# Attention stage of a fused attention and mixture-of-experts kernel: wider fp32 products, clamp and q's product trade engines, loads by chunk

## The chip, the cores and the metric

The kernel runs on one core of one Trainium2 chip. The metric is the device time in microseconds (us) of one execution. The engines of the core are named as in the profile: PE (TensorE: matrix products and transposes), PEld (its weight loads), DVE (VectorE), ACT (ScalarE), POOL (GpSimd) and SP (SyncE, which here issues loads and stores).

## The reference, cut to what matters

A gated linear attention over 4 batches, 8 heads, 768 steps and head size 48 feeds a top-2 mixture of 8 experts (3072 tokens, width 384, inner width 1024), which feeds a feed-forward block with inner width 2048. The attention is the part that the change touches:

```python
f = 1.0 / (1.0 + np.exp(-f_logit))
for t in range(S):
    state = f[:, :, t, :, None] * state + np.einsum('bhd,bhe->bhde', k[:, :, t], v[:, :, t])
    y[:, :, t] = np.einsum('bhd,bhde->bhe', q[:, :, t], state)
```

The rows of y, with the heads side by side, are the tokens x. The logits of the experts are `x @ w_gate + log1p(exp(x @ w_noise)) * noise`; the two largest choose the experts and their weights. An expert is `relu(x @ w1) @ w2`; the last block is `h = x @ w_in; (h - tanh(h)) @ w_out`.

## The kernel before

**Chunks.** The 768 steps are cut into six chunks of 128 for each of four batches: 24 chunks, numbered j, batch fastest. One chunk has f, k and q as [128, 4, 128] tiles (partitions: two heads of 64 rows, 48 of them used; four pairs of heads a; 128 steps) and v as [128 steps, 8 heads, 48]. Per chunk SP loads f (256 KB), kq (512 KB) and v (192 KB).

**The work of one chunk**, by function name. `clamp` bounds f from below (L303; on DVE for the first three chunks, on POOL for the rest). `decay` takes exp and ln on ACT (L310, L311) and a running sum along the steps on DVE (L312). `scaled` takes two exponentials on ACT (L320, L321), multiplies k and q by them on DVE (L323, L325) and copies the last step's decay into `gall` on POOL (L326). `scores` makes the 128x128 products of k and q by head on PE (L338), and DVE masks them into `am` (L340). `key_rows` transposes k on PE (L351), ACT copies it out. `outputs` adds, in PSUM, q times the state (L362, from chunk 4 on) and the masked scores times v (L365), and ACT copies the result to x (L368). `states` makes the product of k and v on PE (L379), DVE adds the old state in two half-partition pieces into `tsum` (L383), POOL multiplies it by the decay into `st` (L384). `x_transposed` and `logits` transpose x and multiply it by the gate weights (L390, L402). The 48 rows of a head's state stand in a 96-column block for each pair of heads; the other half of the block is kept at zero, because the two half sums leave it alone.

**Routing.** After each group of four chunks the generator `route` finds the experts and the slots of its tokens; `advance` runs it in small steps between the other work. It then fills `posts` with eight scatters, two per chunk, that write x to the rows `xs` of the experts. `post(n)` issues up to n of them: each a small memset (L470) and an indirect DMA (L471), both on POOL. At j=19 `post(8)` empties the list, and `load_x` (L153, a POOL DMA) loads the first block of tokens of expert 0.

**Order.** The schedule is written out by hand: each engine runs its instructions in the order of the program and waits at each for its data and its buffers. An iteration j of the main loop (from L498 on) issues the loads of chunk j+3, then `scores(j+1)`, `scaled(j+2)`, `decay(j+3)`, `logits(j-1)`, `outputs(j)`, `key_rows(j+1)`, `states(j)`, `x_transposed(j)`, `clamp(j+4)` and `post(4)`. So on POOL an iteration has the copy for `gall` of chunk j+2, the state product of chunk j, the clamp of chunk j+4 and up to four scatters. Chunks 20 to 23 have no key rows and no new state. In iteration 22 three tiles of the first expert block are transposed (`put_x`, L180), and the first product of an expert (L192) is issued in iteration 23.

PSUM is used by bank names: scores b3 and b4, key rows b1, outputs b5, the key and value product and the warming products b6, logits b7. `warm(n)` issues n small bf16 products (L484) whose result nobody reads; the start has `warm(80)`.

Before the loop the load queue of SP has f of chunks 0 and 1, then for each chunk kq, v and the f two chunks on, the gate weights, and eight writes of zeros (288 KB each, L294) into rows of `xs`. After the loop come the expert stage (L192, L207) and the feed-forward stage (the same lines of products), written out in the same manner.

Of the kernel before, what the change touches and what calls it, by code (L numbers as in the profile page):

```python
# [8 lines left out]
F32 = mybir.dt.float32  # L9
# [14 lines left out]
NT = B * NCH  # L24
# [35 lines left out]
def fast(ctx, tc, flag, f_cols, kq_cols, v_rows, gates, w12, w_in, w_out, out):  # L60
# [34 lines left out]

    gall = consts.tile([128, NT, 4], F32, name="gall")
    yslot = consts.tile([128, 2, NT], I32, name="yslot")
# [154 lines left out]
    with ExitStack() as actx:  # L252
# [11 lines left out]
        def load_all(j):  # L264
            if j < NT:
                t = loads.tile([128, 2, 4, 128], F32, name="kq")
                nc.sync.dma_start(t.rearrange("p n a t -> p (n a t)"), kq_cols[j])
                T["k", j], T["q", j] = t[:, 0], t[:, 1]
                T["v", j] = loads.tile([128, H, D], F32, name="v", bufs=4)
                nc.sync.dma_start(T["v", j].rearrange("p h d -> p (h d)"), v_rows[j])  # L270
            load_f(j + 2)

        load_f(0)
        load_f(1)
        load_all(0)
        load_all(1)
        gn = small.tile([128, GN], F32, name="gn", bufs=1)
        nc.sync.dma_start(gn, gates)
        wgn = gn[:, 0:48].rearrange("p (a c) -> p a c", a=3)
        nz = gn[:, 48:].rearrange("p (c b e) -> p c b e", c=NCH, b=B)  # L280
        load_all(2)

        carry = acst.tile([128, 4, 128], F32, name="carry")
        nc.vector.memset(carry, 1.0)
        nc.vector.memset(carry[:, :, 0:1], 0.0)
        st = acst.tile([128, B, 4, 96], F32, name="st")
        nc.vector.memset(st, 0.0)
        tsum = acst.tile([128, 4, 96], F32, name="tsum")
        nc.vector.memset(tsum, 0.0)
        spare = gath.tile([128, 4, DM], F32, name="x4", bufs=2)  # L290
        empty = spare[:(CAP - FILLED) // 4].rearrange("p a d -> p (a d)")
        nc.vector.memset(empty, 0.0)
        for e in range(NE):
            nc.sync.dma_start(rows(xs, (NE * 512 + e * 320 + FILLED - 512) * DM, [[4 * DM, (CAP - FILLED) // 4], [1, 4 * DM]]),  # L294
                              empty)
# [3 lines left out]
        def clamp(j):  # L299
            if j >= NT:  # L300
                return
            fc = work.tile([128, 512], F32, name="fc")
            (nc.vector if j < 3 else nc.gpsimd).tensor_scalar(fc, T.pop(("f", j)), FMIN, None, op0=OP.max)  # L303
            T["fc", j] = fc
# [9 lines left out]
        def scaled(j):  # L314
            if j >= NT:
# [8 lines left out]
                                           op0=OP.min, op1=OP.mult)  # L324
            nc.vector.tensor_tensor(t[:, 1], eneg, T.pop(("q", j)), op=OP.mult)  # L325
            nc.gpsimd.tensor_copy(gall[:, j, :], eneg[:, :, 127])  # L326
            T["kT", j], T["qT", j] = t[:, 0], t[:, 1]
# [28 lines left out]
        def outputs(j):  # L356
            c, b = divmod(j, B)
            am, qT, vt = T.pop(("am", j)), T.pop(("qT", j)), T["v", j]
            pY = ps.tile([128, H, D], F32, name="pY", tag="b5")
            for a in range(4):  # L360
                if c:
                    nc.tensor.matmul(pY[:, 2 * a:2 * a + 2, :].rearrange("p h d -> p (h d)"), qT[:, a, :],  # L362
                                     st[:, b, a, :], start=True, stop=False)
                for s in range(2):
                    nc.tensor.matmul(pY[:, 2 * a + s, :], am[:, s, a, :], vt[:, 2 * a + s, :],  # L365
                                     start=not c, stop=bool(s) or not c)
            x = xkeep[j // 4 % 3][:, j % 4, :]
            nc.scalar.activation(x, pY.rearrange("p h d -> p (h d)"), AF.Copy)  # L368
            T["x", j] = x

        def states(j):
# [6 lines left out]
            for a in range(4):  # L378
                nc.tensor.matmul(pK[:, a, :], k[:, a, :], vt[:, 2 * a:2 * a + 2, :].rearrange("p h d -> p (h d)"),  # L379
                                 start=True, stop=True)  # L380
            for s in range(2):
                pp, cc = slice(64 * s, 64 * s + 64), slice(48 * s, 48 * s + 48)
                nc.vector.tensor_tensor(tsum[pp, :, cc], pK[pp, :, cc], st[pp, b, :, cc], op=OP.add)  # L383
            nc.gpsimd.tensor_tensor(st[:, b], tsum, gall[:, j, :, None].to_broadcast([128, 4, 96]), op=OP.mult)  # L384

# [12 lines left out]
        def logits(j):  # L398
            p = ps.tile([128, 16], F32, name="pt", tag="b7")
            xT = T.pop(("xT", j))  # L400
            for a in range(3):
                nc.tensor.matmul(p, xT[:, a, :], wgn[:, a, :], start=(a == 0), stop=(a == 2))  # L402
            nc.scalar.activation(lgs[:, j, :], p, AF.Copy)

# [76 lines left out]
        def warm(n):  # L481
            p = ps.tile([128, 512], F32, name="pK", tag="b6")
            for _ in range(n):
                nc.tensor.matmul(p[:, :128], ones, ones, start=True, stop=True)  # L484

        clamp(0)
        decay(0)
        warm(80)
        clamp(1)
        scaled(0)  # L490
        decay(1)
        scores(0)
        key_rows(0)
        scaled(1)
        clamp(2)
        decay(2)
        clamp(3)
        for j in range(NT):  # L498
            load_all(j + 3)
            rate = 2 if j < NT - 1 else 8  # L500
            scores(j + 1)
# [21 lines left out]
            clamp(j + 4)  # L523
            post(4)
            advance(rate)
# [192 lines left out]
    def check_routes():  # L718
        holds(0, gall.rearrange("p a b -> p (a b)"), GMIN, OP.is_ge)
        holds(1, dv, 0.0, OP.is_lt)  # L720
# [327 lines left out]
```

## Time and profile before

| | |
|---|---|
| median of 3 runs | 1092.74 us (1091.09 to 1095.36) |
| profiled execution | 1092.13 us, its span 1090.1 us |
| mean granted clock of TensorE | 0.958 |
| PE busy | 1059.0 us, 97% of the span |
| PEld busy | 980.8 us, 90% |
| DVE busy | 637.4 us, 58% |
| ACT busy | 501.3 us, 46% |
| POOL busy | 183.8 us, 17% |
| moved by DMA | 115.31 MB, mean 106 GB/s |

The profile is of one execution. The span runs from the first to the last instruction. In a row of busy time by stretch the length is followed by the busy us of PE, PEld, DVE, ACT and POOL, each with its number of instructions in parentheses. A matrix product of fp32 operands stands in the trace as two instructions, and so does its weight load; a transpose is one. PEclk, or the granted clock, is the share of TensorE's full clock of 2.4 GHz that was granted in a stretch: 1.00 is 2.4 GHz, 0.50 is 1.2 GHz. In a row of a timeline the first number is the start, the second the duration of the merged instructions, and a bracket gives the engine's idle time before them with what ended it. POOL's scatters count as instructions of POOL; what the DMA moves afterwards does not.

### The profile page before, as it was taken

Reading aid. Unit: us, or ns where it says so; the run is one execution under the profiler, and the core shown is the slowest. Engines: PE = TensorE matmul, PEld = TensorE weight load, DVE = VectorE, ACT = ScalarE, POOL = GpSimd, SP = SyncE. Lnnn points to the kernel's source line nnn. Section 1 sums busy time; section 2 is a strip of 40 time slices with the busy share of each in tenths; the row PEclk is TensorE's granted clock in tenths of the full one; section 3 lists DMA queues with packets and bytes.
Section 4 is the critical chain, followed back from the end, with each engine's and each line's share of the span. In section 5 each row is a group of like instructions: output and inputs, shape, how many; then the busy total and the mean of one; then the engine's idle time right before and its main releaser. Section 6 shows DMA issues by size and latency. Waiting matters only on the chain.

```text
span 1090.1 us, 16283 instructions
## 1 busy us (share of the span) xinstructions
PE 1059.0 (97%) x6170; PEld 980.8 (90%) x6170; DVE 637.4 (58%) x1285; ACT 501.3 (46%) x1017; POOL 183.8 (17%) x246
## 2 busy tenths in 40 slices
PE   7989888999999999999999999999999999999997
PEld 7889887899998989999999998998999989999996
DVE  6866665335555555556666576656655555555543
ACT  4654544233242434334444444554655555555552
POOL 2466666430000000000000011410201101000000
PEclk7988777799999999999999999999999999999998
DMA  8665554253453535354445343310101111000000
GB/s 252 233 213 165 169 187 143 97 152 111 117 185 102 168 108 167 115 170 130 149 119 155 96 143 109 94 30 30 51 13 53 30 37 45 1 29 1 29 1 33
DMA packets 54723, 115.31 MB, mean 106 GB/s; under 512 B 7210, under 2 KB 30510, under 8 KB 54637
## 3 DMA queue, kind: packets, MB, share of 16 engines
q1 hardware_dynamic: 46140, 85.08, 25.2%
q0 software_dynamic: 8496, 29.11, 8.5%
q8 instruction: 51, 0.84, 0.3%
q14 instruction: 36, 0.29, 0.1%
HBM read 84.27 MB, written 29.88 MB: 105 GB/s over the span
## 4 chain that ended last, share of the span: by engine, by line
PE 90%; POOL 5%; DVE 2%; ACT 2%; issue 1%; POOLq 0%; DVEq 0%
PE py L207 39%; PE ph L192 38%; PE pY L365 3%; PE px L180 3%; POOL fc L303 2%; POOL xs L471 2%; PE pA L338 2%; PE pY L362 1%; PE pK L379 1%; PE pt L402 1%; POOL st L384 1%; PE pE L390 1%; PE pkr L351 1%; DVE tsum L383 1%; ACT fc L310 1%
## 5 line engine op out<-in xcount | busy, mean ns | idle before, releaser
L207 PE MATMUL py<-wsplit,hs 128*128 128x384 f32 x2432 | 462.6, 337 | 0.0
L207 PEld LDWEIGHTS py<-wsplit,hs 128*128 128x128 f32 x2432 | 430.1, 188 | 13.2
L192 PE MATMUL ph<-xtH,wsplit 128*128 128x512 f32 (+3 forms) x768 | 230.9, 359 | 2.0 <-ACT xtH L182 1.5
L192 PE MATMUL ph<-xtH,winS 128*128 128x512 f32 x576 | 196.4, 396 | 0.0
L192 PEld LDWEIGHTS ph<-xtH,wsplit 128*128 128x128 f32 x768 | 140.0, 189 | 15.7 <-ACT xtH L182 1.9
L192 PE MATMUL ph<-xtL,wsplit 128*128 128x320 f32 (+3 forms) x384 | 135.3, 352 | 0.0
L619 DVE SCALAR_TENSOR_TENSOR s<-s,z 128x512 f32<-128x512 f32 x96 | 66.5, 692 | 109.8 <-ACT s L618 109.2
L192 PEld LDWEIGHTS ph<-xtH,winS 128*128 128x128 f32 x576 | 108.1, 188 | 20.4
L216 ACT ACTIVATE hs<-ph 128x512 fp32r<-128x512 f32 (+3 forms) x128 | 66.0, 516 | 129.7 <-PE ph L192 103.5
L627 ACT ACTIVATE hs<-g 128x512 fp32r<-128x512 f32 x96 | 60.7, 632 | 140.4 <-DVE g L621 138.9
L220 DVE SCALAR_TENSOR_TENSOR hs<-ph,hs 128x256 fp32r<-128x256 f32 (+2 forms) x192 | 79.6, 443 | 75.7 <-ACT hs L216 69.8
L192 PE MATMUL ph<-xtL,winS 128*128 128x512 f32 x288 | 113.4, 394 | 0.0
L628 DVE TENSOR_TENSOR hs<-g,hs 128x512 fp32r<-128x512 f32 x96 | 66.5, 693 | 63.6 <-ACT hs L627 62.9
L126 DVE TENSOR_TENSOR wsplit<-raw,wsplit 128x768 fp32r<-128x768 f32 x72 | 69.3, 963 | 39.2 <-ACT wsplit L125 38.9
L183 DVE TENSOR_TENSOR xtL<-px,xtH 128x384 fp32r<-128x384 f32 (+1 forms) x80 | 42.8, 536 | 62.5 <-ACT xtH L182 55.3
L192 PEld LDWEIGHTS ph<-xtL,wsplit 128*128 128x128 f32 x384 | 72.7, 189 | 5.8 <-DVE xtL L183 0.3
L617 ACT ACTIVATE z<-ph 128x512 f32<-128x512 f32 x96 | 57.3, 596 | 43.0 <-PE ph L192 41.4
L125 ACT ACTIVATE wsplit<-raw 128x768 fp32r<-128x768 f32 x72 | 60.5, 840 | 27.7 <-DMA raw<-in_w 27.6
L618 ACT ACTIVATE s<-z,bias_a 128x512 f32<-128x512 f32 x96 | 69.7, 726 | 3.1
L182 ACT ACTIVATE xtH<-px 128x384 fp32r<-128x384 f32 (+1 forms) x80 | 37.6, 471 | 72.1 <-PE px L180 71.6
L621 DVE TENSOR_TENSOR g<-s,ph 128x512 f32<-128x512 f32 x96 | 65.9, 687 | 3.3
L153 POOL DMA_DIRECT2D x<-xs x16 | 8.9, 556 | 343.5 <-PE px L180 341.3
(124 smaller groups left out, 1185.1 us busy)
## 6 DMA issues: line engine op xcount, KB each, us to landing
raw<-in_w SPq DMA_DIRECT2D x64, 384.0 KB
kq<-in_kq_cols SPq DMA_DIRECT2D x24, 512.0 KB
y_rows<-yo SPq DMA_DIRECT2D x41, 192.0 KB
f<-in_f_cols SPq DMA_DIRECT2D x24, 256.0 KB
w<-in_moe_w_out SPq DMA_DIRECT2D x32, 192.0 KB
w<-in_moe_w_in SPq DMA_DIRECT2D x24, 256.0 KB
v<-in_v_rows SPq DMA_DIRECT2D x24, 192.0 KB
x<-xs POOLq DMA_DIRECT2D x6, 768.0 KB
```

What stands on the lines that cost most here:

```text
L125: nc.scalar.activation(t[:, 0], raw, AF.Copy)
L126: nc.vector.tensor_tensor(t[:, 1], raw, t[:, 0].bitcast(F32), op=OP.subtract)
L192: nc.tensor.matmul(ph[:, :n], l, r[:, a, :n], start=(o == 0), stop=(o == 8))
L207: nc.tensor.matmul(p[:max(m, 128)], l, r, start=(f == 0 and o == 0), stop=(f == last and o == len(ops) - 1))
L216: nc.scalar.activation(hs[:, :n], ph[:, :n], AF.Relu)
L220: nc.vector.scalar_tensor_tensor(hs[:, at:at + hi - lo], ph[:, lo:hi], 0.0, hs[:, lo:hi].bitcast(F32), op0=OP.max, op1=OP.subtract)
L617: nc.scalar.activation(z, ph, AF.Square, accum_out=hsum[:, i:i + 1])
L618: nc.scalar.activation(s, z, AF.Square, bias=bias_a)
L619: nc.vector.scalar_tensor_tensor(s, s, ZD, z, op0=OP.add, op1=OP.mult)
L621: nc.vector.tensor_tensor(g, s, ph, op=OP.mult)
L627: nc.scalar.activation(hs[:, :512], g, AF.Copy)
L628: nc.vector.tensor_tensor(hs[:, 512:], g, hs[:, :512].bitcast(F32), op=OP.subtract)
```

## The change

**Wider products.** `outputs` streams 144 columns of the state instead of 96, and gives each product of masked scores the 48 columns of v twice, to its own place and to a place that a later product overwrites or nobody reads. `logits` streams 96 columns of the gate tile instead of 16 and copies the first 16. The state of a batch is a tile of its own with 432 columns.

**Engines.** All clamps are on DVE. q's product (L325) is on POOL, ahead of the decay column. The decay column becomes a product with a mask `own`, so that the unused halves of the state blocks are multiplied by zero; the state sum is then one instruction over all partitions.

**Order.** f, kq and v are loaded chunk by chunk; chunk 2 and the gate weights come later in the program. The clearing of the state tiles, the first three clamps and the first decays are put in another order; `warm(10)` stands before the loop and at the top of iterations 1 and 2. The writes of zeros are issued two each in iterations 1 to 4. Up to iteration 19 `post` issues two scatters instead of four.

**Check.** The test of the smallest decay first takes the larger of the two masked columns.

```diff
@@ -93,7 +93,7 @@
 
-    gall = consts.tile([128, NT, 4], F32, name="gall")
+    gall = consts.tile([128, NT, 4, 2], F32, name="gall")
     yslot = consts.tile([128, 2, NT], I32, name="yslot")
@@ -268,29 +268,29 @@
                 nc.sync.dma_start(T["v", j].rearrange("p h d -> p (h d)"), v_rows[j])
-            load_f(j + 2)
+            if j:
+                load_f(j + 1)
 
         load_f(0)
+        load_all(0)
         load_f(1)
-        load_all(0)
         load_all(1)
         gn = small.tile([128, GN], F32, name="gn", bufs=1)
-        nc.sync.dma_start(gn, gates)
         wgn = gn[:, 0:48].rearrange("p (a c) -> p a c", a=3)
         nz = gn[:, 48:].rearrange("p (c b e) -> p c b e", c=NCH, b=B)
-        load_all(2)
 
         carry = acst.tile([128, 4, 128], F32, name="carry")
         nc.vector.memset(carry, 1.0)
         nc.vector.memset(carry[:, :, 0:1], 0.0)
-        st = acst.tile([128, B, 4, 96], F32, name="st")
-        nc.vector.memset(st, 0.0)
-        tsum = acst.tile([128, 4, 96], F32, name="tsum")
-        nc.vector.memset(tsum, 0.0)
+        own = acst.tile([128, 2], F32, name="own")
+        nc.vector.memset(own, 0.0)
+        for s in range(2):
+            nc.vector.memset(own[64 * s:64 * s + 64, s:s + 1], 1.0)
+        st = [acst.tile([128, 432], F32, name=f"st{b}") for b in range(B)]
         spare = gath.tile([128, 4, DM], F32, name="x4", bufs=2)
         empty = spare[:(CAP - FILLED) // 4].rearrange("p a d -> p (a d)")
-        nc.vector.memset(empty, 0.0)
-        for e in range(NE):
+
+        def clear(e):
             nc.sync.dma_start(rows(xs, (NE * 512 + e * 320 + FILLED - 512) * DM, [[4 * DM, (CAP - FILLED) // 4], [1, 4 * DM]]),
@@ -300,7 +300,7 @@
             fc = work.tile([128, 512], F32, name="fc")
-            (nc.vector if j < 3 else nc.gpsimd).tensor_scalar(fc, T.pop(("f", j)), FMIN, None, op0=OP.max)
+            nc.vector.tensor_scalar(fc, T.pop(("f", j)), FMIN, None, op0=OP.max)
             T["fc", j] = fc
@@ -322,8 +322,9 @@
                                            op0=OP.min, op1=OP.mult)
-            nc.vector.tensor_tensor(t[:, 1], eneg, T.pop(("q", j)), op=OP.mult)
-            nc.gpsimd.tensor_copy(gall[:, j, :], eneg[:, :, 127])
+            nc.gpsimd.tensor_tensor(t[:, 1], eneg, T.pop(("q", j)), op=OP.mult)
+            nc.gpsimd.tensor_tensor(gall[:, j], eneg[:, :, 127:128].to_broadcast([128, 4, 2]),
+                                    own[:, None, :].to_broadcast([128, 4, 2]), op=OP.mult)
             T["kT", j], T["qT", j] = t[:, 0], t[:, 1]
@@ -356,16 +357,19 @@
             am, qT, vt = T.pop(("am", j)), T.pop(("qT", j)), T["v", j]
-            pY = ps.tile([128, H, D], F32, name="pY", tag="b5")
+            pY = ps.tile([128, 512], F32, name="pY", tag="b5")
+
             for a in range(4):
+                at = 96 * a
                 if c:
-                    nc.tensor.matmul(pY[:, 2 * a:2 * a + 2, :].rearrange("p h d -> p (h d)"), qT[:, a, :],
-                                     st[:, b, a, :], start=True, stop=False)
+                    nc.tensor.matmul(pY[:, at:at + 144], qT[:, a, :], st[b][:, at:at + 144], start=True, stop=False)
                 for s in range(2):
-                    nc.tensor.matmul(pY[:, 2 * a + s, :], am[:, s, a, :], vt[:, 2 * a + s, :],
+                    two = pY[:, at + 48 * s:at + 48 * s + 96].rearrange("p (n d) -> p n d", n=2)
+                    two = bass.AP(tensor=two.tensor, offset=two.offset, ap=[two.ap[0], [96 - 48 * s, 2], two.ap[2]])
+                    nc.tensor.matmul(two, am[:, s, a, :], vt[:, 2 * a + s, None, :].to_broadcast([128, 2, D]),
                                      start=not c, stop=bool(s) or not c)
             x = xkeep[j // 4 % 3][:, j % 4, :]
-            nc.scalar.activation(x, pY.rearrange("p h d -> p (h d)"), AF.Copy)
+            nc.scalar.activation(x, pY[:, :384], AF.Copy)
             T["x", j] = x
@@ -378,10 +382,11 @@
                                  start=True, stop=True)
-            for s in range(2):
-                pp, cc = slice(64 * s, 64 * s + 64), slice(48 * s, 48 * s + 48)
-                nc.vector.tensor_tensor(tsum[pp, :, cc], pK[pp, :, cc], st[pp, b, :, cc], op=OP.add)
-            nc.gpsimd.tensor_tensor(st[:, b], tsum, gall[:, j, :, None].to_broadcast([128, 4, 96]), op=OP.mult)
+            tsum = work.tile([128, 4, 96], F32, name="tsum")
+            nc.vector.tensor_tensor(tsum, pK, st[b][:, :384].rearrange("p (a d) -> p a d", a=4), op=OP.add)
+            nc.gpsimd.tensor_tensor(st[b][:, :384].rearrange("p (a s d) -> p a s d", a=4, s=2),
+                                    tsum.rearrange("p a (s d) -> p a s d", s=2),
+                                    gall[:, j, :, :, None].to_broadcast([128, 4, 2, D]), op=OP.mult)
 
@@ -396,11 +401,11 @@
         def logits(j):
-            p = ps.tile([128, 16], F32, name="pt", tag="b7")
+            p = ps.tile([128, 96], F32, name="pt", tag="b7")
             xT = T.pop(("xT", j))
             for a in range(3):
-                nc.tensor.matmul(p, xT[:, a, :], wgn[:, a, :], start=(a == 0), stop=(a == 2))
-            nc.scalar.activation(lgs[:, j, :], p, AF.Copy)
+                nc.tensor.matmul(p, xT[:, a, :], gn[:, 16 * a:16 * a + 96], start=(a == 0), stop=(a == 2))
+            nc.scalar.activation(lgs[:, j, :], p[:, :16], AF.Copy)
 
@@ -483,20 +488,31 @@
 
+        warm(85)
         clamp(0)
+        clamp(1)
         decay(0)
-        warm(80)
-        clamp(1)
+        for s_ in st:
+            nc.vector.memset(s_, 0.0)
+        decay(1)
+        load_all(2)
+        nc.sync.dma_start(gn, gates)
         scaled(0)
-        decay(1)
+        clamp(2)
+        scaled(1)
         scores(0)
-        key_rows(0)
-        scaled(1)
-        clamp(2)
         decay(2)
         clamp(3)
+        key_rows(0)
+        warm(10)
+        nc.vector.memset(empty, 0.0)
         for j in range(NT):
             load_all(j + 3)
+            if j in (1, 2, 3, 4):
+                clear(2 * j - 2)
+                clear(2 * j - 1)
+            if j in (1, 2):
+                warm(10)
             rate = 2 if j < NT - 1 else 8
@@ -521,7 +537,7 @@
             clamp(j + 4)
-            post(4)
+            post(2 if j < 20 else 4)
             advance(rate)
@@ -716,7 +732,9 @@
     def check_routes():
-        holds(0, gall.rearrange("p a b -> p (a b)"), GMIN, OP.is_ge)
+        least = small.tile([128, NT * 4], F32, name="least", bufs=1)
+        nc.vector.tensor_reduce(least, gall.rearrange("p j a s -> p (j a) s"), axis=AX.X, op=OP.max)
+        holds(0, least, GMIN, OP.is_ge)
         holds(1, dv, 0.0, OP.is_lt)
```

## Rows read from the trace of the kernel before

**Rows 1.** Busy time by stretch: us, five engines (x instructions), PEclk, DMA share, GB/s

```profile
0.00:30.25 30.25, 23.59 (x200) 22.15 (x200) 21.16 (x36) 15.03 (x26) 5.91 (x14) 0.77 0.89 263
30.25:41.23 10.98, 10.88 (x107) 10.14 (x106) 8.34 (x14) 7.46 (x16) 5.09 (x6) 1.00 0.75 255
41.23:165.16 123.93, 114.12 (x925) 107.81 (x924) 86.85 (x198) 64.39 (x135) 76.62 (x93) 0.82 0.55 181
165.16:205.18 40.02, 33.94 (x220) 31.02 (x220) 17.93 (x45) 12.89 (x29) 25.31 (x41) 0.68 0.39 137
205.18:1090.10 884.92, 876.49 (x4724) 809.67 (x4722) 503.11 (x995) 401.51 (x811) 70.87 (x92) 1.00 0.28 87
```

**Rows 2.** The same view of three single iterations, j=8 to j=10

```profile
69.38:78.94 9.56, 6.80 (x63) 6.18 (x62) 4.97 (x14) 4.19 (x10) 8.73 (x12) 0.91 0.79 236
78.94:90.79 11.85, 11.85 (x64) 11.29 (x63) 8.56 (x26) 4.68 (x9) 5.88 (x9) 0.50 0.35 136
90.79:97.02 6.23, 6.23 (x62) 6.00 (x61) 4.24 (x8) 3.91 (x8) 2.78 (x3) 0.99 0.50 160
```

**Rows 3.** Waits in the attention stage: us in total, times, longest us

```profile
ACT fc L310 <- POOL spacer L470: 24.8, 8, 4.8
ACT fc L310 <- POOL fc L303: 24.3, 12, 3.9
```

**Rows 4.** Timeline of PE, 60 to 92 us: start, us, instructions [idle before]

```profile
63.16 1.16 PE L338 MATMUL pA<-kqT 64*128 64x128 f32 x16
...
67.23 0.57 PE L365 MATMUL pY<-v,am 128*128 128x48 f32 x4
67.64 0.62 PE L351 MATMUL pkr<-ident,kqT 128*128 128x128 f32 x4
68.09 1.03 PE L379 MATMUL pK<-v,krows 128*128 128x96 f32 x8
68.96 0.49 PE L390 MATMUL pE<-ident,xkeep 128*128 128x128 f32 x3
...
78.11 0.90 PE L390 MATMUL pE<-ident,xkeep 128*128 128x128 f32 x3 [2.76 <-ACT xkeep L368]
```

**Rows 5.** Timeline of POOL, 45 to 95 us

```profile
64.72 2.19 POOL L303 TENSOR_SCALAR fc<-f 128x512 f32<-128x512 f32 x1
...
67.13 1.47 POOL L471 DMA_INDIRECT xs<-xkeep,yslot  x1 [0.18 <-issue]
...
73.30 0.20 POOL L326 COPY gall<-eneg 128x4 f32<-128x4 f32 x1
```

**Rows 6.** Groups of the attention stage by line: busy us, mean ns, idle before

```profile
L303 POOL TENSOR_SCALAR fc<-f 128x512 f32<-128x512 f32 x21 | 36.7, 1749 | 0.0
...
L325 DVE TENSOR_TENSOR kqT<-eneg,kq 128x512 f32<-128x512 f32 x24 | 17.7, 736 | 0.0
L384 POOL TENSOR_TENSOR st<-tsum,gall 128x384 f32<-128x384 f32 x20 | 16.6, 829 | 56.6 <-DVE tsum L383 56.6
...
L303 DVE TENSOR_SCALAR fc<-f 128x512 f32<-128x512 f32 x3 | 1.6, 530 | 0.0
...
L287 DVE MEMSET st<- 128x1536 f32 x1 | 1.3, 1338 | 0.3 <-issue 0.3
```

**Rows 7.** Timeline of PE at the start

```profile
10.82 1.16 PE L338 MATMUL pA<-kqT 64*128 64x128 f32 x16 [2.96 <-DVE kqT L325]
...
15.20 2.08 PE L338 MATMUL pA<-kqT 64*128 64x128 f32 x16 [2.63 <-DVE kqT L325]
```

**Rows 8.** Timeline of POOL at the end of the attention stage

```profile
185.67 0.59 POOL L153 DMA_DIRECT2D x<-xs  x1 [2.19 <-DMA xs<-xkeep,yslot]
```

**Rows 9.** Timeline of PE at the end of the attention stage

```profile
179.94 0.90 PE L390 MATMUL pE<-ident,xkeep 128*128 128x128 f32 x3 [4.08 <-ACT xkeep L368]
...
203.68 0.69 PE L192 MATMUL ph<-xtH,wsplit 128*128 128x384 f32 x1 [1.46 <-ACT xtH L182]
```

**Rows 10.** The page's costliest group, over the whole span

```profile
L207 PE MATMUL py<-wsplit,hs 128*128 128x384 f32 x2432 | 462.6, 337 | 0.0
```

## Prediction

> **What bounds the kernel now.** Busy time by stretch comes first. [rows 1] cut the 1090.1 us span at starts of loop iterations (an iteration j begins with the scores of chunk j+1). From 205.18 us on TensorE (PE) is busy 876.5 of 884.9 us at full clock: the expert and feed-forward stages, which the diff leaves as they are. All that can move lies in the first 205 us, the attention stage: a start to the beginning of iteration j=2 (30.25 us), iterations 2 and 3 (10.98 us for two), iterations 4 to 18 (123.93 us for fifteen, 8.26 us each, mean clock 0.82), and a tail of 40.02 us (clock 0.68).
>
> Next the same view of single iterations [rows 2]. An undisturbed one takes 6.23 us with PE busy throughout at clock 0.99. The one that begins at 69.38 takes 9.56 us, 2.76 of them PE idle, and the next one 11.85 us, fully busy at 0.50, which is 1.2 GHz. So four iterations take 6.22 + 6.22 + 9.56 + 11.85 = 33.9 us where four of the first kind would take 24.9. The pattern comes back with the scatters of each group of four chunks.
>
> The waits say who causes it [rows 3]: ScalarE's exponential of the decay (L310) waits 24.3 us in 12 waits for GpSimd's clamp (L303) and 24.8 us in 8 waits for the tiny memset (L470) ahead of a scatter, which stands directly behind a clamp on GpSimd (POOL), so that this too is the clamp. The consequence is PE's gap of 2.76 us ahead of 78.11 [rows 4]: the transpose of x waits for the copy of x, which stands behind that exponential on ScalarE. POOL's queue gives the reason [rows 5]: clamp 64.72, then four scatters from 67.13 to 73.30 (1.54 us each), only then the next chunk's work, and four more scatters after the next clamp. The clamp is early in code and late in the queue.
>
> **The change, part by part.** Durations are of the profiled execution: span 1090.1 us, its own time 1092.1, the median of three runs 1092.7, so the profiled one stands for the median.
>
> *The clamp goes to VectorE (DVE), q's product to POOL.* POOL loses 1.749 us per chunk [rows 6]. What it gains has no row on POOL. Lower bound: the state product (128x384) took 0.829 us, by elements 0.829 x 512/384 = 1.1 us for 128x512. Upper bound: the slowest clamp shown, 2.19 us [rows 5]. I take 1.3, nearest to the same operation kind. DVE loses 0.736 and gains 0.530 (the three clamps that it does now): 0.2 us less. The clamp then stands behind the state sum on DVE, with no scatter ahead of it: the L310 waits of [rows 3] go.
>
> What is late next is q's product: it stands behind the state product and the scatters on POOL, and the scores wait for it.
>
> *Two scatters per iteration instead of four in two of four.* A group of four chunks makes eight, so two per iteration just keep up. POOL per iteration: state product 0.83 + two scatters 3.08 + q's product 1.3 + the decay column 0.2 (0.20 from 73.30 to its end; now a masked product of 8 elements, at most the 0.83 of the big one) = 5.4 us, with the upper bounds 6.9. PE needs 6.2, so by the middle values POOL keeps up. The loop through both engines: from the start of the scores to the end of the key product is 68.96 - 63.16 = 5.80 us on PE [rows 4], then the state sum (no row of that shape on DVE; POOL's 0.83 for the same shape is taken), state product 0.83, two scatters 3.08, q's product 1.3: 11.8 us. That product feeds the scores two iterations on, so the loop allows 5.9 us per iteration, 6.4 with the upper bound for q's product. Both are near PE's own pace, so I add a little jitter.
>
> *Wider products.* A value product streams 96 columns instead of 48, the state product 144 instead of 96, the logits 96 instead of 16. In records each fp32 product is two passes. At full clock 48 columns take (67.64 - 67.23)/4 = 0.103 us per pass, 96 columns (68.96 - 68.09)/8 = 0.109 [rows 4]: the passes go at nearly one pace whatever they stream. 16 passes x 0.006 = 0.1 us per chunk, and for 8 passes at 144 columns, which no row shows, another 0.05 by the same slope (nothing to 0.2). I take 0.15.
>
> The Trainium skill (TensorE: Matmul & The Clock Gate, section Back-to-back issue gap) has a gap that grows with the columns, N/2.4 ns plus 2.5: by it 48 columns more would cost 20 ns per pass and the chunk 16 x 0.020 + 8 x 0.020 + 6 x 0.033 = 0.68 us. The trace shows 6 ns for 48 columns, so here the rule's slope is hidden; it returns as a rival, priced by another row.
>
> So an iteration from 4 to 18 is PE's 6.22 + 0.15 = 6.37, taken as 6.4: 15 x (8.26 - 6.4) = 27.9 us gained. Iterations 2 and 3 hold no stall; they lose 2 x 0.15 = 0.3.
>
> *State sum in one piece, state tiles, zeroing.* One 128x384 sum instead of two half sums on DVE, under PE's cover; at most the 0.83 us that POOL takes for that shape.
>
> *The start.* Loads now come as f, kq, v of a chunk. The first clamp needs 256 KB; the second, for f of chunk 1, needs 256 + 512 + 192 + 256 KB = 1.25 MB, which at the 263 GB/s of the first stretch [rows 1] takes 4.7 us, some 5.5 to 6.5 us on the clock. On DVE the order is clamp 0, clamp 1, scan 0, the clearing of four state tiles (1.3 us, as one memset now [rows 6]), scan 1, the product with k for chunk 0: the first scores come near 11.5 us, where they begin at 10.82 now [rows 7]. Then less is in the way: the second scores wait 2.63 us now [rows 7], and chunk 1 is already scanned in the new order. The eight zero-row writes leave the front of the load queue. Against it: thirty extra warming products, and those of iterations 1 and 2 write the PSUM bank (tag b6) that the state sum of the iteration before must first have read, so that PE waits there for DVE's last operation; that bank is the new wait, about 1 us per iteration, with all of the next scores queued behind it. Put together iteration 2 begins at 28.5 (26 to 31) against 30.25: 1.75 gained. The zero rows go out in iterations 1 to 4, 8 x 288 KB, 576 KB beside 960 KB of loads per iteration, 1.57 MB in 6.2 us or 254 GB/s, which the first stretch has moved; cost nothing, and a late f if that cover is gone.
>
> *The tail.* After iteration 19 begins POOL has the state product of chunk 19 at about +6.7 us, then all six scatters left of group 3 (two, then post(8)): 6 x 1.54 = 9.2, then load_x, which waits for their landing (2.19 us now, 0.59 of its own [rows 8]), and only then q's product for chunk 22: 6.7 + 0.8 + 9.2 + 2.8 + 1.3 = 20.8 us. PE gets to those scores after 6.2 + 4.9 (an iteration without key transposes, 0.45, and key product, 0.87) = 11.1. So a gap of 9.7 us opens here, in place of today's 4.08 [rows 9]. After it: iteration 21 at half clock 9.8, iteration 22 with three x transposes at full clock 6.2, the wait for the transposed x 1.46 [rows 9], the first expert block 1.5: 20.8 + 9.8 + 6.2 + 1.5 + 1.5 = 39.8 against 40.02. Full clock at once would make it 34.9, half clock to the end 47. Taken: 0.2 gained.
>
> Sum: 1.75 - 0.3 + 27.9 + 0.2 = 29.55 us off 1092.1: **1062.5 us**.
>
> **The rivals.**
>
> *A. POOL and DVE hold each other up.* For: POOL's clamp averages 1.75 and took 2.19 us while DVE was at work [rows 5, 6]; q's product is one more POOL operation that reads two operands. Against: a DVE product averages 0.736, hardly stretched [rows 6]. Price: POOL at its upper bound, 6.9, and a little waiting: 7.2 us per iteration, 15 x 0.8 = 12 more: 1074. The Trainium skill (SBUF — State Buffer, section SBUF: two separate sides) says that the two share a port pair as an exclusive lock, taken for a whole instruction, also where DVE has two SBUF inputs and GpSimd reads SBUF. The lengthened clamp bears out that they contend, not that one blocks fully.
>
> *B. The columns are paid.* A pass of the expert and feed-forward stages with 384 columns takes 462.6/2432 = 0.19 us, 0.5 ns per column [rows 10]. If a narrow pass paid that for each column it gains, the chunk would cost 16 x 48 + 8 x 48 + 6 x 80 = 1632 columns, 0.8 us instead of 0.15: 0.65 more in some 20 iterations, 13 us: 1075. Against: the two paces of [rows 4]. The gap rule of the Trainium skill, named above, points this way.
>
> *C. The wait only changes its name.* q's product stands behind the scatters as the clamp does now, and the stalls every four iterations stay. Only the clamp waits before the scatters begin (about 3 us, an estimate) and the 1.75 of the start are gained: 1087. Against: half as many scatters stand ahead of it.
>
> *D. Slower.* If q's product ends over 1.5 us late in every iteration (POOL near 7.7 us instead of 5.4), PE has a gap each time; a gap of 2.76 us dropped the clock to 0.50 and an iteration to 11.85 us [rows 2, 4]. Its place is the wait of the scores for q's product; it decides from an iteration of 8.4 us, where the gain is used up. All fifteen at 11.85 would cost 15 x 3.6 = 54 us; half of them 27: 1092 + 27 = about 1117. Against: it needs q's product above 3 us, beyond the bound.
>
> **How the numbers follow.** Forecast 0.55, A 0.2, B 0.1, C 0.08, D 0.07. The forecast's own range is 1052 to 1069 (start 2.5 either way, pace 6.2 to 6.6, tail 5 down, 7 up). With A and B inside, and a tail and start that both turn out well below, the range is 1048 to 1081. A measurement of this kernel tells about 0.5%, 5.5 us, from no change: faster by more than that 0.86 (forecast, A, B and a little of C), within it 0.06, slower 0.08.
>
> **What would show it.** Right: no L310 wait on POOL in iterations 4 to 18, clock near 1.00 from 30 to 140 us, iterations of 6.2 to 6.6 us, q's product on POOL at 1.1 to 2.2 us, a PE gap over 5 us behind load_x, passes at 96 columns near 0.11 us. Wrong: PE waiting for q's product in most iterations (A or D), passes near 0.12 us or more (B), a start of iteration 2 after 31 us, or the clock at 0.50 for long stretches before the tail.

## The result, and the profile after

The changed kernel took 1064.01 us (median of four runs, 1063.46 to 1064.79) against 1092.18 us beside it, a ratio of 0.9738 [0.9716, 0.976]. The profiled execution took 1064.79 us with a span of 1063.0. So the profiled gain is 27.1 us of span.

Busy time by stretch of the kernel after, cut at the same iterations as [rows 1]; columns as there:

```profile
0.00:31.34 31.34, 23.17 (x236) 21.74 (x236) 20.36 (x39) 15.90 (x29) 11.73 (x17) 0.89 0.62 207
31.34:42.03 10.69, 10.69 (x108) 10.12 (x106) 7.54 (x11) 6.74 (x15) 4.58 (x6) 1.00 0.87 256
42.03:139.59 97.56, 95.73 (x925) 90.93 (x924) 85.98 (x183) 64.60 (x136) 70.50 (x93) 1.00 0.73 243
139.59:177.85 38.26, 26.51 (x219) 23.95 (x220) 15.74 (x41) 12.51 (x29) 24.91 (x43) 0.85 0.40 146
177.85:1063.00 885.15, 876.69 (x4724) 811.46 (x4722) 504.00 (x996) 401.83 (x811) 71.66 (x92) 1.00 0.28 87
```

Against [rows 1] the start lost 1.09 us, iterations 2 and 3 gained 0.29, iterations 4 to 18 gained 26.37, the tail gained 1.76 and the rest lost 0.23: 27.1 in all. The clock of iterations 4 to 18 went from 0.82 to 1.00, and an iteration takes 97.56/15 = 6.50 us.

Waits of the attention stage, in the form of [rows 3]:

```profile
PE pA L339 <- POOL kqT L325: 8.0, 7, 6.2
ACT fc L310 <- DVE fc L303: 7.6, 5, 3.5
```

Both waits of [rows 3] are gone: the exponential waits for DVE 7.6 us in all, and no longer for POOL. New is the wait of the scores for q's product. PE's timeline shows where, in the form of [rows 4], [rows 7] and [rows 9]:

```profile
14.51 2.08 PE L339 MATMUL pA<-kqT 64*128 64x128 f32 x16 [6.25 <-POOL gall L326]
...
24.30 0.72 PE L489 MATMUL pK<-ones 128*128 128x128 bf16 x10 [0.52 <-DVE tsum L386]
...
65.29 0.58 PE L369 MATMUL pY<-v,am 128*128 128x96 f32 x4
65.71 0.60 PE L352 MATMUL pkr<-ident,kqT 128*128 128x128 f32 x4
...
106.64 1.16 PE L339 MATMUL pA<-kqT 64*128 64x128 f32 x16 [0.20 <-POOL kqT L325]
113.44 1.16 PE L339 MATMUL pA<-kqT 64*128 64x128 f32 x16 [0.40 <-POOL kqT L325]
119.76 1.16 PE L339 MATMUL pA<-kqT 64*128 64x128 f32 x16
...
158.64 2.08 PE L339 MATMUL pA<-kqT 64*128 64x128 f32 x16 [6.16 <-POOL kqT L325]
...
166.44 1.16 PE L339 MATMUL pA<-kqT 64*128 64x128 f32 x16
...
176.35 0.55 PE L192 MATMUL ph<-xtH,wsplit 128*128 128x384 f32 x1 [1.76 <-issue]
```

The first scores start 3.7 us later than in [rows 7]. In the loop, waits of 0.20 and 0.40 us stand where [rows 4] had 2.76. Behind the load of x a gap of 6.16 us has opened. POOL's timeline gives its reason:

```profile
11.17 2.65 POOL L325 TENSOR_TENSOR kqT<-eneg,kq 128x512 f32<-128x512 f32 x1 [9.88 <-DMA f<-in_f_cols]
...
147.12 1.02 POOL L476 DMA_INDIRECT xs<-xkeep,yslot  x1 [0.16 <-issue]
...
153.60 0.97 POOL L476 DMA_INDIRECT xs<-xkeep,yslot  x1 [0.23 <-issue]
156.70 0.59 POOL L153 DMA_DIRECT2D x<-xs  x1 [2.13 <-DMA xs<-xkeep,yslot]
157.31 1.28 POOL L325 TENSOR_TENSOR kqT<-eneg,kq 128x512 f32<-128x512 f32 x1
```

Six scatters, the load of x that waits for their landing, and only then q's product, for which the scores at 158.64 wait. The groups that answer to [rows 6]:

```profile
L325 POOL TENSOR_TENSOR kqT<-eneg,kq 128x512 f32<-128x512 f32 x24 | 32.8, 1366 | 16.7 <-DMA f<-in_f_cols 9.9 <-ACT eneg L321 6.5
...
L387 POOL TENSOR_TENSOR st<-tsum,gall 128x384 f32<-128x384 f32 x20 | 18.3, 916 | 31.4 <-DVE tsum L386 31.4
...
L386 DVE TENSOR_TENSOR tsum<-pK,st 128x384 f32<-128x384 f32 x20 | 11.1, 555 | 10.1 <-PE pK L383 7.5 <-POOL gall L326 2.6
L303 DVE TENSOR_SCALAR fc<-f 128x512 f32<-128x512 f32 x24 | 10.0, 416 | 5.3 <-DMA f<-in_f_cols 5.3
```

q's product costs POOL 1.37 us where the clamp cost 1.75, and the clamp costs DVE 0.42 where q's product cost 0.74.

### The profile page after: what moved, and what is told of

It reads as the page before. It is cut to its first block, busy times and chain, and to the rows that moved or that the text cites. A ratio compares the mean times of both kernels' runs of the same rounds, so it can differ in the third digit from the quotient of the medians.

```text
span 1063.0 us, 16296 instructions
## 1 busy us (share of the span) xinstructions
PE 1032.8 (97%) x6205; PEld 958.2 (90%) x6205; DVE 633.6 (60%) x1268; ACT 501.6 (47%) x1017; POOL 183.4 (17%) x249
## 4 chain that ended last, share of the span: by engine, by line
PE 93%; POOL 3%; issue 1%; DVE 1%; DMA 1%; SPq 0%; ACT 0%; POOLq 0%; DVEq 0%
PE py L207 40%; PE ph L192 39%; PE pY L369 3%; PE pA L339 2%; PE px L180 2%; PE pY L365 2%; PE pt L407 2%; POOL xs L476 1%; PE pK L383 1%; POOL kqT L325 1%; DMA f<-in_f_cols 1%; PE pkr L352 0%; PE pE L395 0%; POOL st L387 0%; DVE tsum L386 0%
## 5 line engine op out<-in xcount | busy, mean ns | idle before, releaser
L633 ACT ACTIVATE z<-ph 128x512 f32<-128x512 f32 x96 | 57.2, 596 | 41.1 <-PE ph L192 39.8
```

Of the source, the lines that this page charges most:

```text
L633: nc.scalar.activation(z, ph, AF.Square, accum_out=hsum[:, i:i + 1])
```

## The experiments

Ratios are to the kernel before on the same chip. "After" and "before" in front of a diff name the kernel that is edited.

**1. The trade alone** (before):

```diff
-            (nc.vector if j < 3 else nc.gpsimd).tensor_scalar(fc, T.pop(("f", j)), FMIN, None, op0=OP.max)
+            nc.vector.tensor_scalar(fc, T.pop(("f", j)), FMIN, None, op0=OP.max)
-            nc.vector.tensor_tensor(t[:, 1], eneg, T.pop(("q", j)), op=OP.mult)
+            nc.gpsimd.tensor_tensor(t[:, 1], eneg, T.pop(("q", j)), op=OP.mult)
```

> The kernel before with only the trade: all clamps on VectorE, q's product on GpSimd, four scatters per iteration as before. If the trade were the remedy for the waits: iterations 4 to 18 near 6.4 us, 1070 us or less. If q's product only takes the clamp's place behind the scatters: GpSimd has 0.83 + 6.2 + 1.3 + 0.2 = 8.5 us in two iterations of four, PE waits for q's product at the scores in each group, the clock falls there for some 12 us with narrow products: 1085 to 1095 us.

1095.73 us, ratio 0.9994 [0.9981, 1.0007]: nothing. PE's timeline:

```profile
69.65 1.16 PE L338 MATMUL pA<-kqT 64*128 64x128 f32 x16 [2.91 <-POOL kqT L325]
102.23 2.08 PE L338 MATMUL pA<-kqT 64*128 64x128 f32 x16 [2.72 <-POOL kqT L325]
```

and POOL's:

```profile
62.40 1.67 POOL L471 DMA_INDIRECT xs<-xkeep,yslot  x1 [0.18 <-issue]
...
67.34 0.96 POOL L471 DMA_INDIRECT xs<-xkeep,yslot  x1 [0.22 <-issue]
68.32 1.28 POOL L325 TENSOR_TENSOR kqT<-eneg,kq 128x512 f32<-128x512 f32 x1
```

and the iteration from 102.23 by busy time:

```profile
102.23:113.98 11.75, 11.74 (x62) 11.19 (x62) 5.89 (x15) 2.02 (x6) 6.67 (x12) 0.50 0.40 143
```

Four such gaps of 2.7 to 3.2 us stand ahead of iterations 8, 12, 16 and 20, and each of these iterations took 10.2 to 11.75 us, the second at 0.50 throughout. This is the stall of rival C: q's product now stands behind the four scatters, where the clamp stood.

**2. The clamp alone** (before; the first pair of lines of the diff above and nothing else):

> The kernel before with one line changed: all clamps on VectorE; q's product stays there too, four scatters per iteration, narrow products, old start. If the wait on GpSimd's clamp is the whole loss: no group gap, iterations 4 to 18 at 6.2 to 6.4 us, the tail gap gone, ratio to before 0.965 to 0.972 (1092 - 31 to 38 us). If bursts of scatters hold up GpSimd's state product, or VectorE (0.4 us more per iteration, two half sums kept) becomes the bound: ratio 0.98 or more.

1046.8 us, ratio 0.9591 [0.9564, 0.9617], below what both theories named, and faster than the whole change. By stretch:

```profile
0.00:29.09 29.09, 22.06 (x200) 20.78 (x201) 20.36 (x37) 15.31 (x27) 2.37 (x12) 0.88 0.86 252
...
39.74:134.52 94.78, 93.96 (x924) 89.42 (x924) 92.19 (x211) 65.94 (x136) 48.80 (x78) 1.00 0.74 237
134.52:161.00 26.48, 23.83 (x221) 21.72 (x222) 20.49 (x48) 12.97 (x29) 16.95 (x30) 1.00 0.46 162
```

With four scatters, narrow products and the old order, an iteration takes 6.32 us at full clock and the tail 26.48. DVE is busy 92.19 of 94.78 us and still keeps up. What still stands behind the scatters on POOL, the decay column and the state product, is first read by PE four chunks later.

**3. q's product on DVE in the changed kernel**, for all chunks, and in another kernel for chunks 22 and 23 alone (after):

```diff
-            nc.gpsimd.tensor_tensor(t[:, 1], eneg, T.pop(("q", j)), op=OP.mult)
+            nc.vector.tensor_tensor(t[:, 1], eneg, T.pop(("q", j)), op=OP.mult)
```

> The changed kernel with q's product of every chunk on VectorE; the clamp stays there too, so GpSimd has only the state product, the decay column and the scatters. If VectorE keeps under PE's 6.33 us: no gap per group and none in the tail, 1048 to 1051 us. If VectorE becomes the bound (0.7 us more per iteration): pace 6.6 us or more, 1055 us or more.

1049.45 us, ratio 0.9569 [0.9551, 0.9587].

```profile
0.00:29.38 29.38, 22.41 (x235) 20.96 (x236) 21.66 (x43) 16.01 (x29) 4.36 (x13) 0.94 0.67 221
...
40.08:135.34 95.26, 95.26 (x924) 90.94 (x924) 88.03 (x197) 64.51 (x135) 57.94 (x78) 1.00 0.75 249
135.34:163.18 27.84, 24.30 (x222) 22.09 (x222) 17.72 (x45) 12.71 (x29) 19.31 (x33) 1.00 0.49 178
```

PE is busy in all of 95.26 us. Of the 15.6 us of span against the change, the tail gives 38.26 - 27.84 = 10.42, iterations 4 to 18 give 2.30, the start 1.96. The other kernel, `nc.gpsimd if j < 22 else nc.vector`:

> The changed kernel with q's product of chunks 22 and 23 alone on VectorE. If the 6.16 us gap in the tail stands there only because that product is queued behind the scatters and load_x on GpSimd: the gap goes, and with it 2 us each of half clock after it; the first expert product begins some 9 us earlier: 1053 to 1056 us. If the transfer of load_x or the routing is late there anyway: 1060 to 1064 us.

1051.4 us, ratio 0.9584 [0.9566, 0.9602]. Its tail:

```profile
139.60:166.54 26.94, 24.30 (x221) 22.09 (x222) 16.98 (x43) 12.35 (x29) 17.88 (x32) 1.00 0.46 169
```

Two chunks of 24 give back 38.26 - 26.94 = 11.3 us: the price of q's product on POOL is nearly all in the gap behind the load of x and in the half clock after it. The rest of the difference is within the intervals. The time is some 2 us below the range of the first expectation.

**4. The trade undone in the changed kernel** (after; experiment 1's diff reversed):

> The changed kernel with the clamp back on GpSimd (from chunk 3 on) and q's product back on VectorE. If the trade of engines is what removed the waits: L310 waits for the clamp return, PE gaps and half clock with them, 1075 us or more. If two scatters per iteration suffice: iterations 4 to 18 stay near 6.4 us, and the 6.16 us gap behind load_x in the tail, which waits for q's product on GpSimd, goes with its half clock: 1064 - 8 = 1056 us.

1052.49 us, ratio 0.9649 [0.9623, 0.9675], faster than the change. The theory that only the trade removes the loss fell here. The exponential still waits for POOL, but for 1.9 us at most where [rows 3] has 4.8: with two scatters in front of it, the clamp on POOL is late by less.

```profile
ACT fc L310 <- POOL spacer L475: 18.9, 14, 1.9
```

```profile
103.89 0.18 PE L441 MATMUL pt<-sel,before 128*128 128x32 bf16 x1 [0.80 <-ACT lgs L408]
```

PE's gaps of 0.5 to 0.8 us, as the one ahead of 103.89, come once in four iterations, and the clock stayed at full after them:

```profile
104.00:116.00 12.00, 12.00 (x119) 11.42 (x118) 9.72 (x21) 7.78 (x16) 10.41 (x13) 1.00 0.65 220
```

**5. The same with narrow products** (experiment 4 with the state product at 96, values at 48 and logits at 16 columns):

```diff
-                    nc.tensor.matmul(pY[:, at:at + 144], qT[:, a, :], st[b][:, at:at + 144], start=True, stop=False)
+                    nc.tensor.matmul(pY[:, at:at + 96], qT[:, a, :], st[b][:, at:at + 96], start=True, stop=False)
...
-                    nc.tensor.matmul(two, am[:, s, a, :], vt[:, 2 * a + s, None, :].to_broadcast([128, 2, D]),
+                    nc.tensor.matmul(pY[:, at + 48 * s:at + 48 * s + 48], am[:, s, a, :], vt[:, 2 * a + s, :],
...
-                nc.tensor.matmul(p, xT[:, a, :], gn[:, 16 * a:16 * a + 96], start=(a == 0), stop=(a == 2))
+                nc.tensor.matmul(p[:, :16], xT[:, a, :], wgn[:, a, :], start=(a == 0), stop=(a == 2))
```

> The changed kernel with the clamp on GpSimd, q's product on VectorE (as in the run trade_back) and narrow products. If columns matter only after gaps of over a microsecond and the 0.8 us gap per group of trade_back is harmless with narrow products too: 0.1 us less per iteration, 1050 to 1053 us. If narrow products let the clock fall at that gap, as in the run with two scatters alone: half-clock stretches of 12 us or more, 1060 to 1070 us.

1064.71 us, ratio 0.9702 [0.9681, 0.9723], some 0.5% above experiment 4. Gaps of the same kind:

```profile
79.83 0.19 PE L439 MATMUL pt<-sel,before 128*128 128x32 bf16 x1 [0.88 <-DVE kqT L325]
107.40 0.18 PE L439 MATMUL pt<-sel,before 128*128 128x32 bf16 x1 [0.89 <-ACT fc L311]
```

```profile
79.80:84.00 4.20, 4.17 (x31) 3.84 (x32) 2.99 (x12) 1.65 (x4) 2.56 (x4) 0.59 0.38 133
...
108.00:130.00 22.00, 22.00 (x220) 20.84 (x220) 18.45 (x42) 15.19 (x32) 18.53 (x24) 1.00 0.67 229
```

After the gap ahead of 79.83 the clock fell, after the like one at 107.40 it did not; in experiment 4 it fell after none. The profiled execution is the slowest of four (1068.09). Of its 16.5 us of span above experiment 4's, 102.76 - 98.61 = 4.15 us lie in iterations 4 to 18 and 36.88 - 28.19 = 8.7 in the tail, where its clock was 0.50 from 156 to 180 us and experiment 4's 1.00; so the gaps of the loop are the smaller part of the difference.

**6. Narrow products in the change, and wide ones in the kernel before** (after with experiment 5's diff; before with the change's wider products alone):

> The changed kernel with its narrow products back (48, 96 and 16 columns instead of 96, 144 and 96), all else as changed. Theory W (the gain is the wait on the clamp that went; no PE gap, so no loss of clock in iterations 4 to 18): those iterations stay at 6.3 to 6.5 us at clock 1.00; columns count only after a gap, at the start and in the tail, where the half clock lasted 4.7 and 4.3 us after PE went on, against 10.8 and 13 us or more before: some 7 us in all, 1071 us. Theory C (the columns hold the clock up): the clock falls to 0.50 for long stretches in iterations 4 to 18 too, 1080 us or more. Theory N (columns do nothing to the clock): 1062 to 1064 us.

1064.76 us, ratio 0.9758 [0.9733, 0.9783]: no difference that can be told from the change's 0.9738. Its loop and tail, the stretch behind its load of x, and at the end the changed kernel behind its own gap:

```profile
40.22:137.24 97.02, 94.08 (x924) 89.25 (x923) 86.40 (x183) 64.93 (x137) 70.54 (x93) 1.00 0.75 245
137.24:179.79 42.55, 33.35 (x221) 30.68 (x222) 15.87 (x41) 12.52 (x29) 24.97 (x43) 0.68 0.37 135
```

```profile
150.00:178.00 28.00, 20.91 (x109) 19.34 (x109) 5.77 (x17) 4.07 (x10) 13.90 (x25) 0.52 0.25 99
```

```profile
152.00:180.00 28.00, 17.86 (x123) 15.93 (x124) 6.23 (x18) 5.30 (x13) 14.03 (x27) 0.76 0.26 100
```

The loop ran at full clock without the wide products, as theory W has it. Behind the load of x the clock was at the lower level for some 28 us (150 to 178); with wide products it was there for two spells, 153 to 163 and 177 to 179.5. So the tail is 4.3 us longer. The start of this execution, 1.8 us shorter, iterations 4 to 18, 0.5 shorter, and the stages behind the tail, 2.0 shorter (1062.9 - 179.79 against 885.15), give it back.

> The kernel before with only the wider products. The gaps on the clamp stay, four of about 2.8 us or more. Theory W with columns that shorten the half clock after a gap: each half-clock stretch falls from about 13 to 4.5 us, 4.2 us each for four of them, the tail some 9, the start 3: 1092 - 29 = 1063 to 1072 us, about as much as the whole change. Theory N: no effect, 1092 to 1094 us. If columns are paid (0.65 us per chunk): above 1095 us.

1075.18 us, ratio 0.9851 [0.9827, 0.9875]. PE's gaps stayed:

```profile
76.34 0.55 PE L393 MATMUL pE<-ident,xkeep 128*128 128x128 f32 x3 [2.34 <-ACT xkeep L370]
84.80 0.18 PE L439 MATMUL pt<-sel,before 128*128 128x32 bf16 x1 [3.22 <-ACT lgs L406]
```

By busy time the clock was 1.00 from 76.4 to 85, 0.66 from 85 to 90 and 1.00 again from 90: some 4 us at the lower level after the second gap and nothing after the first, where [rows 2] has a whole iteration of 11.85 us at 0.50. Gaps of 2.27 us ahead of 109.17 and 2.30 ahead of 140.47 were also followed by some 4 us at the lower level, gaps of 1.29 (53.47) and 1.63 (117.64) by none. The expectation that wide products alone bring nearly everything fell.

**7. Two scatters per iteration alone** (before):

```diff
-            post(4)
+            post(2 if j < 20 else 4)
```

> The kernel before with two scatters per iteration instead of four up to iteration 19, nothing else. If the bursts of four scatters make the clamp late: the three stalls with scatters in iterations 8, 12 and 16 go, pace 6.3 us there, the early one near 52 us stays and so does the tail: 1092 - 24 = 1066 to 1072 us. If the clamp has to leave GpSimd for that: stalls stay, 1085 us or more.

1070.26 us, ratio 0.9802 [0.9778, 0.9826]; the profiled execution was the slowest of five (1077.48), so its rows show the kind of loss and not its mean size. The time lies in the range of the first expectation, but not for its reason: the stalls did not go. The exponential still waits for POOL, and now PE's routing product waits for the copy of the logits behind it on ScalarE:

```profile
80.50 0.18 PE L436 MATMUL pt<-sel,before 128*128 128x32 bf16 x1 [1.66 <-ACT lgs L403]
```

```profile
80.50:96.50 16.00, 16.00 (x86) 15.11 (x87) 7.54 (x20) 5.65 (x12) 7.90 (x12) 0.50 0.36 117
```

In this execution iterations 4 to 18 took 122.61 us (41.23 to 163.84, clock 0.80), hardly less than the 123.93 of [rows 1]; the tail, which was expected to stay, took 28.32 us (clock 0.98) instead of 40.02.

**8. What is left to gain beside the clamp**: experiment 3's first kernel with narrow products, with `post(4)` throughout, and without the three `warm(10)` (the diffs above; the last deletes the lines `warm(10)`).

> The run both_dve (ratio 0.957) with narrow products. It has no gap of a microsecond between 30 and 140 us. If columns matter to the clock only where PE has a gap: 0.1 us less per iteration, 1.6 us gained, against some half clock after the gaps of 0.5 to 1.0 us in the tail, 0 to 8 us: ratio 0.955 to 0.963. If narrow products let the clock fall without a gap: 0.97 or more.

> The run both_dve with four scatters per iteration again. Nothing that PE waits for soon is behind them on GpSimd then (the state product is needed four iterations later): the same as both_dve within 0.3%, ratio 0.954 to 0.960. If the bursts hold up PE in another way (the state sum's buffers, DMA traffic): 0.965 or more.

> The run both_dve without the thirty extra warming products. In both_dve PE waits 1.55 and 0.32 us for the state sum before those of iterations 1 and 2, and they take 0.65 us each. If that wait is all they do: iteration 2 begins some 2 us earlier, ratio 0.955. If they hold the clock up at the start: half clock lasts longer there, 2 to 6 us lost, ratio 0.959 to 0.963.

1045.56 us, 0.9581 [0.9558, 0.9603]; 1047.17 us, 0.9594 [0.9567, 0.9621]; 1044.22 us, 0.9575 [0.955, 0.9599]. None can be told from the others, nor from the one line of experiment 2. The profiles show differences that the ratios do not resolve. Narrow products, loop:

```profile
40.05:133.64 93.59, 93.59 (x924) 89.25 (x924) 87.71 (x197) 64.56 (x135) 57.90 (x78) 1.00 0.75 254
```

Without the warming products, start:

```profile
0.00:26.59 26.59, 21.12 (x206) 19.78 (x206) 20.73 (x42) 14.97 (x26) 6.48 (x12) 0.94 0.69 230
```

The wide products cost (95.26 - 93.59)/15 = 0.11 us an iteration. Without the thirty warming products the start of the profiled execution is 29.38 - 26.59 = 2.8 us shorter; counted from the first scores (12.23 and 12.89) it is 17.15 - 13.70 = 3.45 us, by these two executions the price of the products and their waits. The loop was at full clock without them.

## Why the prediction was right, step by step

**The sum** gave 1062.5 us and the profiled execution took 1064.79. The size came from the step that was to bring it: the L310 waits on POOL, PE's gaps and the half clock behind them are gone from iterations 4 to 18, 26.4 us against 27.9 forecast. Experiment 2 shows that the clamp is the cause: moving it, and nothing else, removes all of this loss. That the sum came within 2.5 us of the measured gain is in part luck: against the forecast the start gave 2.84 us less and iterations 4 to 18 1.5 less, the tail 1.56 more and iterations 2 and 3 0.6 more.

**The pace** was put at 6.4 and is 6.50. The wider products were taken as 0.15 us and cost 0.11; a value pass at 96 columns takes (65.71 - 65.29)/4 = 0.105 us, at 48 it took 0.103. Rival B does not hold. The gap that the Trainium skill states (TensorE: Matmul & The Clock Gate, section Back-to-back issue gap) would have made it 0.68 by the estimate of the prediction. That section gives the formula for a single product by itself and says that in a stream of weight loads and products, which these are, it counts too little at small sizes and too much at large ones; so the 0.11 speaks against the prediction's use of the formula. The other part is PE's idle time, 97.56 - 95.73 = 1.83 us or 0.12 an iteration: q's product is late by 0.20 and 0.40 us in two of four iterations. Rival A hardly shows: q's product was taken as 1.3 us on POOL, and took 1.37. It stands behind the state product and the scatters there, in the loop through both engines that the prediction put near PE's own pace.

**The tail** was put at 39.8 and is 38.26. The gap behind the load of x opened where it was forecast, with 6.16 us instead of 9.7, and 1.61 more ahead of a transpose of x. The scatters cost less than assumed: from 147.12 to 153.60 they start (153.60 - 147.12)/5 = 1.30 us apart, where [rows 5] gave 1.54. Behind the gap two errors cancel, which is luck: iteration 21 took 166.44 - 158.64 = 7.80 us and not 9.8, because the half clock ended near 163 us; from there to the first expert product it took 176.35 - 166.44 = 9.91 us and not 6.2 + 1.5, with a wait of 1.44 us ahead of the last transposes of the expert block and 1.76 ahead of that product.

**The start** is the step that failed: iteration 2 was to begin at 28.5 us and began at 31.34, past the 31 us that the prediction names as a sign of being wrong; 1.75 us were to be gained, 1.09 were lost. The mis-sized term is the first scores, put near 11.5 us and found at 14.51. From them to iteration 2 the forecast has 28.5 - 11.5 = 17.0 us, and the run 31.34 - 14.51 = 16.83: the rest of the start, with the thirty warming products that the prediction names without a price, was right as a sum. Some 2.3 of the 3.0 us are the arrival of f for chunk 1, put at 5.5 to 6.5 us and at 8.29 in the run. DVE's timeline of the change:

```profile
8.29 0.43 DVE L303 TENSOR_SCALAR fc<-f 128x512 f32<-128x512 f32 x1 [4.40 <-DMA f<-in_f_cols]
...
12.68 1.68 DVE L323 SCALAR_TENSOR_TENSOR kqT<-epos,kq 128x512 f32<-128x512 f32 x1
```

and of experiment 6's first kernel, which has the same start but for the widths:

```profile
6.54 0.43 DVE L303 TENSOR_SCALAR fc<-f 128x512 f32<-128x512 f32 x1 [2.54 <-DMA f<-in_f_cols]
```

In the nine profiles of kernels with this order of loads this clamp starts between 6.25 and 8.29 us; why it varies is not shown. The first scores of experiment 6's kernel start at 12.76, as in the change 6.22 us behind the clamp. With q's product on DVE, in experiment 3, they start 5.71 us behind a clamp at 6.52:

```profile
12.23 1.77 PE L339 MATMUL pA<-kqT 64*128 64x128 f32 x16 [4.01 <-DVE kqT L325]
```

So q's product on POOL makes the first scores 0.5 us later, and most of the 1.96 us that experiment 3 shows for the start is the arrival. The wait for the bank of the state sum came where it was forecast, but took 0.52 us ahead of 24.30 and 0.32 ahead of 30.69, not 1.

**Iterations 2 and 3** were to lose 0.3 and gained 0.29.

**What the prediction did not see** is that it priced the trade as one step. Its argument for the clamp holds without the rest: the clamp alone gives 0.9591, the whole change 0.9738. Its rival C, weighed with 0.08, is the other half of the trade: its stall comes if the scatters stay at four (experiment 1), and what is left of it at two is the gap in the tail. Rival D, q's product late in every iteration, showed in no run; its sum should read 1092 + 27 = 1119, and nothing else rests on it. The remedies overlap. Alone, two scatters give 2.0%, wide products 1.5%, the clamp 4.1%; all of them shorten PE's gaps in the loop and the tail or the half clock behind them, and once the clamp is on DVE and q's product stays there, the others give nothing that can be measured.

What stays open: why the clock fell after some gaps with narrow products and not after others of the same length; the runs only show that with wide products it fell after none of the gaps of 0.5 to 1.63 us in experiments 4 and 6. The place of the zero writes and the order of the loads were not tried by themselves.

## What to carry to other kernels

When a small operation that others wait for stands behind long issues on an in-order engine, move that operation away, and price each half of an exchange by itself: what is put in its place inherits its queue, and the wait changes its name. Here the engine that took the clamp (VectorE in experiment 2) was 97% busy in the loop and PE still waited only 0.8 us in fifteen iterations, so a full engine is no reason by itself for an exchange. Several remedies for one stall do not add up; try the smallest alone first.

## What the runs showed of the hardware

- A product of two operands on POOL took 1.28 us alone (at 157.31) and 2.65 us in the start of the change, while DVE's scan and k product ran; that k product took 1.68 us there and 0.67 in experiment 3, where POOL has no such product. The Trainium skill (SBUF — State Buffer, section SBUF: two separate sides) has the one that starts first hold the shared pair for the whole instruction. The trace agrees that the two lengthen each other; which of them held the pair when it does not show.
- On POOL the clamp, with one tensor operand, took 1.75 us on average (kernel before) and the product with two operands 1.37 (kernel after), though both write 128x512.
- The granted clock behind gaps. With narrow products it was at 0.50 for 16 us after a gap of 1.66 us ahead of 80.50, though PE was busy throughout, and at 1.00 after one of 1.52 us ahead of 53.61 (both experiment 7); it was at 0.50 for 11.75 us at least after a gap of 2.72 us (experiment 1). With wide products it was at full after gaps of 0.8 us (experiment 4), and for some 4 us at the lower level after one of 3.22 us (experiment 6).
